# A hash-attention and SwiGLU kernel: weight words six pieces ahead, another order of the seven products, sums on x and preparing steps redistributed

## The chip, the cores and the metric

The kernel runs on one core of a Trainium2 chip. The metric is device time in microseconds (us), from the first to the last instruction; every execution of a program counts as one run. The engines of the core run beside each other and wait for one another through semaphores: TensorE (PE in the profile) multiplies, VectorE (DVE) and ScalarE (ACT) do elementwise work and empty the matmul banks (PSUM), GpSimd (POOL) and SyncE (SP) mainly issue DMA transfers.

## The reference

Two stages, cut to what matters. First an attention in which a query sees only the keys that have the same 6-bit hash; then a SwiGLU feed-forward block on the result.

```python
q, k, v: (4, 8, 768, 64) float32      # batch, heads, positions, head size
q_bits = (q @ proj > 0);  k_bits = (k @ proj > 0)        # 6 bits each
scores = where(bucket(q_bits) == bucket(k_bits), q @ k.T / 8, -1e9)
attn   = softmax(scores) @ v
x      = attn as (3072, 512)           # heads side by side
g      = x @ w_gate                    # (512, 1536)
out    = (g * sigmoid(g) * (x @ w_val)) @ w_out          # (1536, 512)
```

The input weights of the feed-forward block are float64; the program receives them as pairs of 32-bit words.

## The kernel before

The program is recorded in one order per engine, so what stands earlier in the Python loop stands earlier on its engine. Four things are interleaved.

**Attention.** The work is cut into 16 pairs of heads (four per batch), each in two halves of the queries: a *unit* is one half of one pair. For every unit TensorE makes the scores of six blocks of keys (the hash bits are multiplied on top of the scores in the same bank), ScalarE takes the exponential, VectorE adds the weights up (`add`, L485 and L489), and TensorE multiplies with v (`attend`). In the first half of a pair the next pair's q and k are transposed, in the second half its hash bits are made: ScalarE takes signs (L389), VectorE scales the k bits (L391). In the first four pairs (batch one) nothing else is multiplied; from the fifth pair on each unit also holds a part of the feed-forward block of the batch before.

**Preparing the weights.** The float64 weights come in 36 pieces of 512 KB (`words`). ScalarE scales both words of a piece (L282, L283), VectorE puts the float32 together in three steps (`narrow`), and after four pieces eight sums (`form`, L328) make the operands of a Strassen product, which go to memory and come back when they are wanted. One *preparing step* is one VectorE instruction of this chain. `load_words` keeps four pieces ahead; `words_tile` says where each piece lands, in space that is used otherwise later.

```python

    spots = [hid[:, half, m].rearrange("p f q -> p (f q)") for half in range(2) for m in range(2)]
    early = [as_words(t[:, 0 : 2 * PIECE]) for t in spots]
    early.append(as_words(part(2 * PIECE, at=down_at + 8 * BL)))
    middle = [as_words(t[:, NFP // 2 * HQ : NFP // 2 * HQ + 2 * PIECE]) for t in spots]
    late = [as_words(part(2 * PIECE, at=stage_at + i * 2 * PIECE)) for i in range(4)]

    def words_tile(i):
        if i < 12:
            return early[i % 5]
        if i < 24 and i % 6 < 4:
            return middle[i % 6]
        if i >= 24 and i % 6 not in (2, 3):
            return late[i % 6 // 4 * 2 + i % 2]
        return wraw.tile([P, PIECE, 2], I32, tag="words", name="words")

    def load_words(done, queue=nc.gpsimd):
        for i in range(len(words), len(pieces)):
            if i - done > 4:
                break
            words[i] = words_tile(i)
            queue.dma_start(words[i].rearrange("p f w -> p (f w)"), pieces[i][1])
...
    def scale_to(count):
...
        for i in range(progress["scaled"], min(count, free, len(pieces))):
            t, w = words[i], pieces[i][0]
...
            nc.scalar.activation(w, t[:, :, 1].bitcast(FP32), AF.Copy, scale=2.0**-112)
            nc.scalar.activation(t[:, :, 0], top, AF.Copy, scale=2.0**-13 * (1 + 2.0**-17))
...
    def scale_ahead():
        i = progress["piece"]
        scale_to(i + 3)
```

**Up.** x @ w_gate and x @ w_val are made as Strassen products: seven products in place of eight, from sums and differences of the quarters of x and of the weights. `first` holds the eight VectorE differences on x. One `step` is one product for the gate (g = 0) or for the value (g = 1), so 14 steps make a part of the up stage, and one unit holds one such part. Three banks for each g (a, b, c) take the products; products that share a bank add up in it, and what has to be used in between is copied out by ScalarE (L605) or added by VectorE (`plus`, L551). A finished gate tile goes through `gate`: tanh on ScalarE (L533), then VectorE (L534, L538).

```python
    def gate(t, g):

        th = t if t is not g else ffn.tile([P, HQ], FP32, tag="th", name="th", bufs=1)
        nc.scalar.activation(th, g, AF.Tanh, scale=0.5)
        return lambda: nc.vector.scalar_tensor_tensor(out=t, in0=th, scalar=1.0, in1=g,
                                                      op0=ALU.add, op1=ALU.mult)
...
            def step(at):
                n, g = divmod(at, 2)
                my = now[g]
                if at == 0:
                    for name in "cba":
                        for w in range(2):
                            now[w][name] = bank("up")[:, 0:HQ]
                    while first:
                        first.pop(0)()
                block, to, xs = (
                    (A11, "a", [x[j][:, lo] for j in range(2)]),
                    (S1, "b", [x[j][:, hi] for j in range(2)]),
                    (S2, "a", [t2[:, j] for j in range(2)]),
                    (A12, "c", [x[2 + j][:, lo] for j in range(2)]),
                    (S3, "a", [t3[:, j] for j in range(2)]),
                    (S4, "b", [x[2 + j][:, hi] for j in range(2)]),
                    (A22, "a", [t4[:, j] for j in range(2)]),
                )[n]
                w = places[g][:, block, :].rearrange("p (j m) -> p j m", m=P)
                c = my[to]
                product(c, [(w[:, j], xs[j]) for j in range(2)], n in (0, 1, 3))
                spot = ((0, 0), (1, 1), (0, 1), (0, 0), (1, 1), (0, 1), (1, 0))[n]
                if n < 3:
                    nc.scalar.copy(tile_of(g, spot), c)
                elif n < 6:
                    plus(my[spot], my[spot], c)
                    c = my[spot]
                while later and later[0][0] <= at:
                    later.pop(0)[1]()
                if n >= 3 and g == 0:
                    then = gate(tile_of(0, spot) if n == 6 else c, c)
                elif n >= 3:
                    then = lambda: gated(hidden(f + spot[0], spot[1]), now[0][spot], c)
                if n >= 3:
                    later.append((at + (1 if n == 6 else 2), then))
                if n in (3, 6):
                    bring(k0 + 2 + g, n // 6)
                while at == 13 and later:
                    later.pop(0)[1]()

```

**Down** (`po` in the profile) multiplies the gated tiles with w_out, again in seven products; its atoms have size 2.

The loop over units mixes all of this:

```python
    for u in range(0, N, NCH):
        n, half, _ = units[u]
        gating = u >= LATE
...
        for c in range(NCH):
            score(u + c)
            if u == 0 and c in (0, 1, 2, 4):
                prepare_pair(1)
                finish(rest)
            if c == 1 and half == 0 and 0 < n <= NP:
                total(n - 1)
            if c:
                add(u + c)
        if n <= NP:
            finish(waiting)
        if not gating and half == 0:
            steps = front(n + 1)
        if not gating and u > 0:
            prepare_pair(2)
        scale_ahead()
        for c in range(NCH):
            attend(u + c)
        if half == 1 and n + 2 < len(pairs):
            load(n + 2)
        if not gating:
            prepare_pair(2 if u > 0 else 4)
        finish(first)
        prepare_on(2)
        finish(rest)
        prepare_on(2)
        if half == 1 and n >= NP:
            total(n)
        prepare_on(0 if u == LATE else 4 if half or gating else 6)
        if not gating:
            continue
...
        credit += 14 if n < 2 * NP else 15.75
        end = True
        part = 0
        while atoms and (credit > 0 or not end):
            size, atom, end = atoms.pop(0)
            credit -= size
            atom()
            part += size
            if part >= 8:
                finish(waiting)
                if u + NCH == N:
                    finish(first)
            if part < 11:
                prepare_on(size)
            if part > 5:
                scale_ahead()
            for _ in range(size):
                if chores:
                    step = chores.pop(0)
                    chores.extend(step and step() or [])
```

`finish(waiting)` puts the normalisation of a pair's result in (L524); `finish(rest)` puts the k scaling in (L391); `chores` are the next pair's transposes or hash signs, one for each step. `gating` is true from the fifth pair on.

Of the kernel before, what the change touches and what calls it, by code (L numbers as in the profile page):

```python
# [10 lines left out]
I32 = mybir.dt.int32  # L11
# [7 lines left out]
def kernel(  # L19
# [224 lines left out]
    def as_words(t):  # L244
        return t.bitcast(I32).rearrange("p (f w) -> p f w", w=2)

    spots = [hid[:, half, m].rearrange("p f q -> p (f q)") for half in range(2) for m in range(2)]
    early = [as_words(t[:, 0 : 2 * PIECE]) for t in spots]
    early.append(as_words(part(2 * PIECE, at=down_at + 8 * BL)))
    middle = [as_words(t[:, NFP // 2 * HQ : NFP // 2 * HQ + 2 * PIECE]) for t in spots]  # L250
    late = [as_words(part(2 * PIECE, at=stage_at + i * 2 * PIECE)) for i in range(4)]

    def words_tile(i):
        if i < 12:
            return early[i % 5]
        if i < 24 and i % 6 < 4:
            return middle[i % 6]
        if i >= 24 and i % 6 not in (2, 3):
            return late[i % 6 // 4 * 2 + i % 2]
        return wraw.tile([P, PIECE, 2], I32, tag="words", name="words")  # L260

    def load_words(done, queue=nc.gpsimd):
        for i in range(len(words), len(pieces)):
            if i - done > 4:
                break
            words[i] = words_tile(i)
            queue.dma_start(words[i].rearrange("p f w -> p (f w)"), pieces[i][1])

    progress = {"late": False, "piece": 0, "scaled": 0, "blocks": 0}
# [86 lines left out]
    def prepare_on(n):  # L356
        for _ in range(n):
            next(preparing, None)

    load_words(-3, nc.sync)  # L360
    for name, queue in (("q", nc.sync), ("k", nc.gpsimd), ("v", nc.sync)):
        fetch(1, name, queue)
    load_words(-1)


    T = {}
# [186 lines left out]
    def up_strassen(x, b, first):  # L553
# [14 lines left out]
        def both(i):  # L568


            f = 2 * i
            k0 = b * NG + 2 * i
            now = [{}, {}]
            later = []

            def tile_of(g, spot):
                m, half = spot
                t = gate_tile() if g == 0 else hidden(f + m, half)
                now[g][spot] = t
                return t  # L580
# [9 lines that stand above are left out]
                        first.pop(0)()  # L590
                block, to, xs = (
                    (A11, "a", [x[j][:, lo] for j in range(2)]),
                    (S1, "b", [x[j][:, hi] for j in range(2)]),
                    (S2, "a", [t2[:, j] for j in range(2)]),
                    (A12, "c", [x[2 + j][:, lo] for j in range(2)]),
                    (S3, "a", [t3[:, j] for j in range(2)]),
                    (S4, "b", [x[2 + j][:, hi] for j in range(2)]),
                    (A22, "a", [t4[:, j] for j in range(2)]),
                )[n]
                w = places[g][:, block, :].rearrange("p (j m) -> p j m", m=P)  # L600
                c = my[to]
                product(c, [(w[:, j], xs[j]) for j in range(2)], n in (0, 1, 3))
                spot = ((0, 0), (1, 1), (0, 1), (0, 0), (1, 1), (0, 1), (1, 0))[n]
                if n < 3:
                    nc.scalar.copy(tile_of(g, spot), c)  # L605
                elif n < 6:
                    plus(my[spot], my[spot], c)
                    c = my[spot]
                while later and later[0][0] <= at:
                    later.pop(0)[1]()  # L610
                if n >= 3 and g == 0:
                    then = gate(tile_of(0, spot) if n == 6 else c, c)
                elif n >= 3:
                    then = lambda: gated(hidden(f + spot[0], spot[1]), now[0][spot], c)
                if n >= 3:
                    later.append((at + (1 if n == 6 else 2), then))
                if n in (3, 6):
                    bring(k0 + 2 + g, n // 6)
                while at == 13 and later:
                    later.pop(0)[1]()  # L620

            for n in range(2 * NB):
                atoms.append((1, lambda n=n: step(n), n == 2 * NB - 1))
# [95 lines left out]
    def finish(todo):  # L719
        while todo:  # L720
            todo.pop(0)()
# [5 lines left out]
    for u in range(0, N, NCH):  # L727
# [26 lines left out]
        if not gating:  # L754
            prepare_pair(2 if u > 0 else 4)
        finish(first)
        prepare_on(2)
        finish(rest)
        prepare_on(2)
        if half == 1 and n >= NP:  # L760
            total(n)
        prepare_on(0 if u == LATE else 4 if half or gating else 6)
        if not gating:
            continue
        chores = []
# [10 lines left out]
        while atoms and (credit > 0 or not end):  # L776
# [4 lines left out]
            if part >= 8:  # L781
                finish(waiting)
                if u + NCH == N:
                    finish(first)
            if part < 11:
                prepare_on(size)
            if part > 5:
                scale_ahead()
# [41 lines left out]
```

## Time and profile before

| what | value |
|---|---|
| time, median of 3 runs | 1019.64 us (1019.41 to 1020.11) |
| span of the profiled run | 1017.2 us |
| mean granted TensorE clock | 0.998 |
| time of batch one (before the first up product) | 0 to 122.1 us |
| VectorE busy between 20 and 120 us | 84.9 us |
| one unit's scores, 36 instructions | 5.04 us |
| one unit's attend, 24 instructions | 4.04 us |
| one part of up, 14 steps in 56 instructions | 18.26 us |

An instruction group in the profile is named by line, engine and operation, then output <- input by the program's names, then its count; what stands in square brackets is the idle time of the engine just before it and what ended that idle time. `L551 DVE TENSOR_TENSOR c<-c,up` is thus the sum of a bank and a tile of the gate. In stretches of time, each engine's busy microseconds are given with its count of instructions, then the TensorE clock as a share of full speed, the busy share of the DMA engines and the GB/s they moved. Scores are `sc`, the products with v are `av`, the row sums `sum`, the hash products `hps`, transposes `tps`.

### The profile page before, as it was taken

The page shows a single profiled execution, that of the slowest core. Times are in us where ns is not written, and L with a number is a line of the kernel's source. Part 1 is how long each engine was busy: PE and PEld are TensorE (multiplying, and loading weights), DVE is VectorE, ACT ScalarE, POOL GpSimd, SP SyncE. Part 2 cuts the span into 40 slices and gives each one's busy share as a digit, 9 for nine tenths or more (in the row PEclk, how much of TensorE's full clock was granted, in tenths as well). Part 3 has the DMA queues.
Part 4 walks back from the last instruction along what each step waited for, and adds up shares of the span by engine and source line. Part 5 has one row for each costly group of instructions (what it writes and reads, how often), then busy time and mean ns, then how long its engine had stood idle before and what let it go on. Part 6 is the DMA issues. An engine that isn't in the chain of part 4 may idle for free.

```text
span 1017.2 us, 12536 instructions
## 1 busy us (share of the span) xinstructions
PE 1002.9 (99%) x4597; PEld 603.2 (59%) x4597; DVE 576.6 (57%) x959; ACT 419.7 (41%) x921; POOL 98.8 (10%) x192
## 2 busy tenths in 40 slices
PE   9998999999999999999999999999999999999998
PEld 4443455545566775555557676555555787555687
DVE  5789988789684515655455453545557341434421
ACT  7776746475532414535342422535435201222200
POOL 2221222311000000000000000000000000111000
PEclk9999999999999999999999999999999999999999
DMA  7774886674323123333430304242222011323001
GB/s 226 217 245 157 218 242 216 196 221 118 89 73 73 33 52 98 94 101 92 104 90 30 73 22 104 88 101 66 72 81 81 21 37 48 107 83 114 31 26 37
DMA packets 120029, 106.21 MB, mean 104 GB/s; under 512 B 89024, under 2 KB 103360, under 8 KB 119968
## 3 DMA queue, kind: packets, MB, share of 16 engines
q0 software_dynamic: 19104, 73.28, 22.4%
q1 hardware_dynamic: 100064, 31.94, 14.0%
q8 instruction: 36, 0.59, 0.2%
q10 hardware_dynamic: 800, 0.20, 0.1%
q14 instruction: 25, 0.20, 0.1%
HBM read 81.79 MB, written 17.30 MB: 97 GB/s over the span
## 4 chain that ended last, share of the span: by engine, by line
PE 86%; DVE 7%; DMA 2%; SPq 2%; issue 2%; ACT 1%; POOL 0%; DVEq 0%; POOLq 0%
PE up L547 40%; PE po L547 21%; PE sc L457 12%; PE av L471 10%; SPq L515 2%; DMA wo<-wo 1%; DVE acc L489 1%; DVE wo L510 1%; PE sum L502 1%; PE hps L404 1%; DVE room L328 1%; DMA hid<-in_moe_w_val_dram 1%; DVE room L299 1%; PE hps L396 1%; DVE xc L551 1%
## 5 line engine op out<-in xcount | busy, mean ns | idle before, releaser
L547 PE MATMUL up<-xT,room 128*128 128x384 f32 x768 | 263.8, 490 | 1.9 <-DVE xT L551 1.9
L547 PEld LDWEIGHTS up<-xT,room 128*128 128x128 f32 x768 | 143.8, 190 | 112.2 <-issue 14.9
L547 PE MATMUL up<-xc,room 128*128 128x384 f32 x576 | 197.6, 486 | 1.1 <-DVE c L551 1.1
L457 PE MATMUL sc<-qT,kT 64*128 64x384 f32 x768 | 161.8, 496 | 0.4 <-DVE c L534 0.4
L547 PEld LDWEIGHTS up<-xc,room 128*128 128x128 f32 x576 | 109.3, 190 | 77.8 <-DVE c L551 1.7
L551 DVE TENSOR_TENSOR c<-c,up 128x384 f32<-128x384 f32 x72 | 39.7, 551 | 180.0 <-PE up L547 179.5
L489 DVE TENSOR_TENSOR acc<-acc,A 128x768 f32<-128x768 f32 x128 | 122.7, 958 | 15.0 <-ACT A L460 1.6
L313 POOL DMA_DIRECT2D room<-ram x96 | 51.8, 540 | 714.0 <-PE up L547 706.5
L460 ACT ACTIVATE A<-sc 128x384 f32<-128x384 f32 x256 | 105.6, 493 | 6.3 <-PE sc L457 6.2
L457 PEld LDWEIGHTS sc<-qT,kT 64*128 64x128 f32 x768 | 68.5, 187 | 52.9 <-issue 47.9
L677 ACT COPY o<-po 128x256 f32<-128x256 f32 x48 | 17.9, 372 | 197.8 <-PE po L547 197.8
L471 PE MATMUL av<-A,vraw 128*64 128x384 f32 (+1 forms) x512 | 88.2, 486 | 0.0
L533 ACT ACTIVATE th<-c 128x384 f32<-128x384 f32 x72 | 37.6, 523 | 115.4 <-DVE c L534 94.4
L551 DVE TENSOR_TENSOR o<-o,po 128x256 f32<-128x256 f32 x36 | 15.1, 420 | 121.0 <-PE po L547 91.9
L457 PE MATMUL sc<-qb,kb 64*128 64x384 bf16 x384 | 65.7, 324 | 4.9 <-DVE kb L391 4.9
L460 ACT ACTIVATE room<-sc 128x384 f32<-128x384 f32 x128 | 54.4, 490 | 37.3 <-PE sc L457 37.3
L547 PE MATMUL po<-room,hid 128*128 128x256 f32 x288 | 66.2, 379 | 1.5 <-DVE o L551 1.5
L547 PE MATMUL po<-wo,hid 128*128 128x256 f32 x288 | 66.9, 382 | 0.0
L547 PE MATMUL po<-wo,room 128*128 128x256 f32 x288 | 66.3, 380 | 0.0
L605 ACT COPY c<-up 128x384 f32<-128x384 f32 x72 | 34.4, 478 | 75.8 <-PE up L547 75.6
L471 PEld LDWEIGHTS av<-A,vraw 128*64 128x64 f32 x512 | 36.7, 137 | 46.0 <-issue 44.8
L547 PEld LDWEIGHTS po<-wo,hid 128*128 128x128 f32 x288 | 54.1, 190 | 12.1 <-issue 4.9
(110 smaller groups left out, 1004.0 us busy)
## 6 DMA issues: line engine op xcount, KB each, us to landing
room<-ram POOLq DMA_DIRECT2D x48, 512.0 KB, 4.8
room<-ram POOLq DMA_DIRECT2D x48, 384.0 KB, 3.8
vraw<-in_v_dram SPq DMA_DIRECT2D x16, 384.0 KB, 3.3
ram<-room POOLq DMA_DIRECT2D x12, 512.0 KB, 4.6
out_dram<-o SPq DMA_DIRECT2D x48, 128.0 KB, 1.7
qraw<-in_q_dram SPq DMA_DIRECT2D x48, 96.0 KB, 3.2
hid<-in_moe_w_val_dram POOLq DMA_DIRECT2D x9, 512.0 KB, 6.8
acc<-acc SPq DMA_DIRECT2D x96, 48.0 KB, 1.9
```

The source lines that it names most:

```text
L299: nc.vector.scalar_tensor_tensor(out=wi, in0=hi, scalar=-(1 << 31), in1=wi, op0=ALU.bitwise_and, op1=ALU.bitwise_or)
L313: nc.gpsimd.dma_start(places[k % 2][:, PARTS[go], :], ram[k % NG][:, PARTS[go], :])
L457: nc.tensor.matmul(sc[h], x["k", n][rows, ks], x["q", n][rows, qs], start=start, stop=not start)
L460: nc.scalar.activation(weights(u)[:, h, 0:HQ], sc[h], AF.Exp, scale=SCALE)
L471: nc.tensor.matmul(ps[h * D : (h + 1) * D, 0:width], raws["v", n][:, h, c, :], a[:, h, 0:width], start=c == 0, stop=c == NCH - 1)
L489: nc.vector.tensor_tensor(acc[n, half], acc[n, half], a[:, :, 0:HQ], op=ALU.add)
L515: nc.sync.dma_start(t[at : at + BLOCK, half, :], r[g : g + BLOCK, :])
L533: nc.scalar.activation(th, g, AF.Tanh, scale=0.5)
L547: nc.tensor.matmul(ps, a, x, start=start and i == 0, stop=i == len(pairs_) - 1, skip_group_check=True)
L551: nc.vector.tensor_tensor(o, a, b, op=op)
L605: nc.scalar.copy(tile_of(g, spot), c)
L677: nc.scalar.copy(o, c)
```

## The change

Four things are changed. The weight words are loaded up to six pieces ahead (in the last eight pieces four), into eight homes in turn for the first twelve pieces, where there were five; a list `homes` takes the place of `words_tile`. In the up stage the product A12, which needs none of the differences on x, comes second instead of fourth, ahead of the products that need them (S1, S2), so that VectorE has time for the differences; it is finished as soon as it is added to the copy of A11, so its gate follows at once. In the last unit of the attention the eight differences on x are put in two per part instead of all at once. And the preparing steps are moved: in batch one every unit has ten (second halves had eight), all after the k scaling; in the later units there are three in place of four behind the row sums and one part fewer has them.

```diff
--- before.py
+++ after.py
@@ -246,24 +246,20 @@
 
     spots = [hid[:, half, m].rearrange("p f q -> p (f q)") for half in range(2) for m in range(2)]
     early = [as_words(t[:, 0 : 2 * PIECE]) for t in spots]
-    early.append(as_words(part(2 * PIECE, at=down_at + 8 * BL)))
     middle = [as_words(t[:, NFP // 2 * HQ : NFP // 2 * HQ + 2 * PIECE]) for t in spots]
     late = [as_words(part(2 * PIECE, at=stage_at + i * 2 * PIECE)) for i in range(4)]
-
-    def words_tile(i):
-        if i < 12:
-            return early[i % 5]
-        if i < 24 and i % 6 < 4:
-            return middle[i % 6]
-        if i >= 24 and i % 6 not in (2, 3):
-            return late[i % 6 // 4 * 2 + i % 2]
-        return wraw.tile([P, PIECE, 2], I32, tag="words", name="words")
+    beside = as_words(part(2 * PIECE, at=down_at + 8 * BL))
+    turn = [None] * 2 + [beside]
+    homes = [(early + middle)[i % 8] for i in range(12)]
+    homes += middle + turn + middle + turn + late + turn + late[:3]
 
     def load_words(done, queue=nc.gpsimd):
         for i in range(len(words), len(pieces)):
-            if i - done > 4:
+            if i - done > (6 if i < 28 else 4):
                 break
-            words[i] = words_tile(i)
+            words[i] = homes[i]
+            if words[i] is None:
+                words[i] = wraw.tile([P, PIECE, 2], I32, tag="words", name="words")
             queue.dma_start(words[i].rearrange("p f w -> p (f w)"), pieces[i][1])
 
     progress = {"late": False, "piece": 0, "scaled": 0, "blocks": 0}
@@ -357,10 +353,10 @@
         for _ in range(n):
             next(preparing, None)
 
-    load_words(-3, nc.sync)
+    load_words(-5, nc.sync)
     for name, queue in (("q", nc.sync), ("k", nc.gpsimd), ("v", nc.sync)):
         fetch(1, name, queue)
-    load_words(-1)
+    load_words(-3)
 
 
     T = {}
@@ -590,29 +586,30 @@
                         first.pop(0)()
                 block, to, xs = (
                     (A11, "a", [x[j][:, lo] for j in range(2)]),
+                    (A12, "c", [x[2 + j][:, lo] for j in range(2)]),
                     (S1, "b", [x[j][:, hi] for j in range(2)]),
                     (S2, "a", [t2[:, j] for j in range(2)]),
-                    (A12, "c", [x[2 + j][:, lo] for j in range(2)]),
                     (S3, "a", [t3[:, j] for j in range(2)]),
                     (S4, "b", [x[2 + j][:, hi] for j in range(2)]),
                     (A22, "a", [t4[:, j] for j in range(2)]),
                 )[n]
                 w = places[g][:, block, :].rearrange("p (j m) -> p j m", m=P)
                 c = my[to]
-                product(c, [(w[:, j], xs[j]) for j in range(2)], n in (0, 1, 3))
-                spot = ((0, 0), (1, 1), (0, 1), (0, 0), (1, 1), (0, 1), (1, 0))[n]
-                if n < 3:
+                product(c, [(w[:, j], xs[j]) for j in range(2)], n in (0, 1, 2))
+                spot = ((0, 0), (0, 0), (1, 1), (0, 1), (1, 1), (0, 1), (1, 0))[n]
+                if n in (0, 2, 3):
                     nc.scalar.copy(tile_of(g, spot), c)
                 elif n < 6:
                     plus(my[spot], my[spot], c)
                     c = my[spot]
                 while later and later[0][0] <= at:
                     later.pop(0)[1]()
-                if n >= 3 and g == 0:
+                done = n in (1, 4, 5, 6)
+                if done and g == 0:
                     then = gate(tile_of(0, spot) if n == 6 else c, c)
-                elif n >= 3:
+                elif done:
                     then = lambda: gated(hidden(f + spot[0], spot[1]), now[0][spot], c)
-                if n >= 3:
+                if done:
                     later.append((at + (1 if n == 6 else 2), then))
                 if n in (3, 6):
                     bring(k0 + 2 + g, n // 6)
@@ -754,12 +751,11 @@
         if not gating:
             prepare_pair(2 if u > 0 else 4)
         finish(first)
-        prepare_on(2)
         finish(rest)
-        prepare_on(2)
+        prepare_on(4)
         if half == 1 and n >= NP:
             total(n)
-        prepare_on(0 if u == LATE else 4 if half or gating else 6)
+        prepare_on(0 if u == LATE else 3 if gating else 6)
         if not gating:
             continue
         chores = []
@@ -781,8 +777,8 @@
             if part >= 8:
                 finish(waiting)
                 if u + NCH == N:
-                    finish(first)
-            if part < 11:
+                    finish([first.pop(0) for _ in range(min(2, len(first)))])
+            if part < 10:
                 prepare_on(size)
             if part > 5:
                 scale_ahead()
```

## The prediction

> **What bounds the kernel now.** I read the page first (shares of the span), then TensorE's waits, then the chain that ended last, and last the timelines of the places where TensorE waits. The page:
>
> ```profile
> PE 1002.9 (99%) x4597; PEld 603.2 (59%) x4597; DVE 576.6 (57%) x959; ACT 419.7 (41%) x921; POOL 98.8 (10%) x192
> PE 86%; DVE 7%; DMA 2%; SPq 2%; issue 2%; ACT 1%; POOL 0%; DVEq 0%; POOLq 0%
> ```
>
> TensorE has 1017.2 - 1002.9 = 14.3 us of idle time, and the change removes no matmul. So whatever it gains is gap, and whatever it loses is new gap. TensorE's waits name the gaps:
>
> ```profile
> PE sc L457 <- DVE kb L391: 4.9, 2, 3.6
> PE up L547 <- DVE xT L551: 1.9, 1, 1.9
> PE po L547 <- DVE o L551: 1.5, 1, 1.5
> PE up L547 <- DVE c L551: 1.1, 1, 1.1
> PE sc L457 <- DVE c L534: 0.4, 1, 0.4
> ```
>
> Columns: total, times, longest, in us. They sum to 9.8 us; the rest of the 14.3 is head and tail. The 3.6 us gap (84 to 87.5 us) costs more than itself, as the stretches after it show (TensorE's busy time and count first; clock, DMA share and GB/s last):
>
> ```profile
> 84.00:88.00 4.00, 0.53 (x4) 0.39 (x6) 3.77 (x7) 2.70 (x6) 0.00 (x0) 0.97 0.79 311
> 88.00:92.00 4.00, 4.00 (x22) 1.29 (x20) 3.80 (x7) 1.58 (x4) 1.48 (x2) 0.60 0.08 23
> ```
>
> The clock is 0.60 for 4 us. From the bits product to the first score of the next position the timeline has 4.36 us (87.47 to 91.83), for the same work 2.77 us elsewhere (59.97 to 62.74): 1.6 us lost. All that could be won is thus 9.8 + 1.6 = 11.4 us, 1.1%. From 230 us on nearly everything in the chain is TensorE, back to back.
>
> [...] at 84.3 us ScalarE has waited 5.0 us for one piece of weights, and the sign operations behind it are late with it. [...] the trace has 0.60 after the gap of 3.6 us and 1.00 around the gap of 1.9 us at 125 us. [...] That is the crux here: the new order of the seven products leaves less room between an eviction and the product that adds into the same bank.
>
> **Part by part.**
>
> *Words six ahead, and the k bits scaled straight after hashing.* The gap of 3.6 us is a chain: ScalarE waits for words, VectorE's preparing step for ScalarE, the k scaling (L391) stands behind that step, the scores wait for it. Words loaded earlier break the first link. The move of two preparing steps behind the k scaling breaks the third. Worth at most 4.9 + 1.6 = 6.5 us. But batch one then carries 10 steps in each second half in place of 8: 8 more in all, at about 0.56 us (a piece is 3 steps in 2.0 us; a block is 4 pieces and 8 sums of 0.40, so 11.2 us for 20 steps), 4.5 us of VectorE, where it has idle only some 15 us between 20 and 120 us (84.9 busy of 100). I count 65%: **-4.2 us**.
>
> *Product without differences second.* At 125 us the second product (S1) waits 1.9 us for x's differences; A12 needs none and gives 2.6 us (two groups of 1.29) in that place. With the wait at the end of this unit: **-2.3 us**.
>
> *Two sums on x per part, last batch.* The 1.5 us at 830 us is an o sum queued behind eight differences (8 x 0.47 = 3.8 us) on VectorE. Two at a time fit between products of 2.6 us: **-1.4 us**. The 1.1 us wait at 228 us goes too, since units hold fewer steps: **-1.1 us**. Sum of gains: -9.0 us.
>
> *What the new order costs.* S2 and S3 both add into bank "a", and S3 must wait until ScalarE has copied S2. Before, A12 stood between them; now S3 comes right behind: only the other group's product (1.29 us) lies between. Second, A12 now ends early, so its tanh stands on ScalarE ahead of the copies of S1 and S2, and in the second half of a pair ahead of the hash signs too. The order of the changed program shows it: copy, copy, tanh, four k signs, copy S1, two q signs, copy S1, two q signs, copy S2. A steady unit of before is the base (the timeline of ScalarE; start, duration):
>
> ```profile
> 459.14 0.48 ACT L605 COPY hid<-up 128x384 f32<-128x384 f32 x1 [0.81 <-PE up L547]
> 461.41 0.48 ACT L605 COPY c<-up 128x384 f32<-128x384 f32 x1 [1.79 <-PE up L547]
> 461.79 1.16 ACT L389 ACTIVATE kb<-hps,columns 32x384 bf16<-32x384 f32 x2
> 462.97 0.48 ACT L605 COPY hid<-up 128x384 f32<-128x384 f32 x1
> 463.46 1.17 ACT L389 ACTIVATE kb<-hps,columns 32x384 bf16<-32x384 f32 x2
> 464.65 0.48 ACT L605 COPY c<-up 128x384 f32<-128x384 f32 x1
> 466.84 1.16 ACT L389 ACTIVATE qb<-hps,columns 32x384 bf16<-32x384 f32 x2
> 468.03 0.52 ACT L533 ACTIVATE th<-c 128x384 f32<-128x384 f32 x1
> ```
>
> Spacings on ScalarE: copy 0.38, tanh 0.43, a pair of signs 1.17, a piece's two scalings 1.14. Put 0 at 461.41, where step 2's product can be evicted; step k's can at 1.29 (k-2). After the change: sum on VectorE and tanh at 0.63, k signs 1.06 to 3.40, copy S1 to 3.78, q signs to 4.95, copy to 5.33, q signs to 6.50, then the copy of S2, done 0.48 later; S3 starts 0.06 after that, at 7.04. It would have started at 6.25 (467.66). So **0.8 us per second-half unit**. Seven have no scaling in between (the last of the first block, three in each of two more): 7 x 0.78 = **+5.5 us**.
>
> In the first block's units scalings come in between as well (counted in the changed program, from the start of the up stage):
> - Unit 2: two pieces, 2 x 1.14, so 0.78 + 2.3 = **+3.1 us**.
> - Unit 4: one piece among the k signs and three behind S1, 4.6; and the tanh comes 0.9 later, as the reciprocal and five preparing steps stand before its sum on VectorE: 0.8 + 4.6 + 0.9 = **+6.3 us**.
> - Unit 1: VectorE does eight differences, six preparing steps and a transpose before A12's sum. From the base:
>
> ```profile
> 125.29 1.02 DVE L551 TENSOR_TENSOR xc<-xT 128x384 f32<-128x384 f32 x2
> 131.42 0.97 DVE L422 STREAM_TRANSPOSE qT<-qraw 128x768 f32<-128x768 f32 x1
> 134.87 0.55 DVE L551 TENSOR_TENSOR c<-c,up 128x384 f32<-128x384 f32 x1
> ```
>
> 125.3 + 3.8 + 4.0 + 1.0 = 134.1; tanh at 134.7; two copies of S1 to 135.9; three pieces, 3.4, to 139.3; copy of S2 to 139.8. S3 could start at 122.1 + 8 x 1.29 = 132.4: **+7.4 us**.
> - Units 3 and 5: at most one piece behind S1, which fits: +0.2 us.
>
> Sum: 5.5 + 3.1 + 6.3 + 7.4 + 0.2 = 22.5 us. Two of these gaps are surely, a third maybe, long enough for the slow clock: 2 x 1.6 = +3.2 us. The last batch's up stage has neither signs nor scalings, and the copy there is in time (0.54 us after its product against 1.09 allowed).
>
> Total: 1019.6 - 9.0 + 22.5 + 3.2 = 1036.3 us.
>
> **Rivals.** (1) *Gaps go, nothing comes*: 1019.6 - 11.4 = 1008 us. For it: each part names a gap that the profile shows. Against: it takes the copy of S2 to be prompt, while ScalarE's order puts 7 us of work before it. (2) *Batch one becomes VectorE's or the DMA queues'*: six pieces ahead is 2 MB more in the first 120 us, where the DMA share is already 0.5 to 0.98, and VectorE gets 4.5 us more; the gains of batch one vanish and 2 to 5 us of new waits come: about 1040 to 1043 us with the stalls above, 1022 without. (3) *The stalls come but are smaller*, if the words' scalings were done earlier by the longer lead: then only the 5.5 us and part of units 1 and 4 remain, about 1024 us.
>
> **Range.** My sum gives 1036; I shade it to 1035, since unit 1 rests on the longest chain. Mechanism right and the first-block stalls halved: 1026. Everything at its worst: 1043. Range 1024 to 1042. Over 2% slower (1040.0) wants the stalls at full size and no gain in batch one: 0.18. Over 2% faster (999) is more than all gaps: 0.005.
>
> **What would show it.** TensorE should newly wait in "up" for ScalarE's copy (L601 there), some ten waits, nine of them in second halves and the longest in units 1 and 4, 6 to 7 us each, with clock under 1 after them; the waits for kb, xT and o should be gone or small. The first tanh of each up unit should stand ahead of the third copy. If no wait for that copy shows, the new order is free and rival 1 holds.

## The result, and the profile after

The changed kernel takes 1063.45 us (median of four runs, 1063.08 to 1065.11), the kernel before 1019.88 us beside it: ratio 1.043, 95% interval 1.041 to 1.045. It is 43.6 us slower; predicted were 1035 us and a range up to 1042.

The page of the changed kernel, busy time of the engines and shares of the chain that ended last:

```profile
PE 1014.6 (96%) x4597; PEld 604.6 (57%) x4597; DVE 582.9 (55%) x959; ACT 418.3 (39%) x921; POOL 99.5 (9%) x192
PE 82%; DVE 6%; ACT 5%; DMA 3%; SPq 1%; issue 1%; POOL 0%; DVEq 0%; ACTq 0%
```

The same 4597 matmuls are busy 11.7 us longer (1014.6 for 1002.9), and the span of 1061.3 us leaves 46.7 us of idle time where there were 14.3. The longer busy time goes with a lower granted clock, 0.982 for 0.998. ScalarE's share of the chain has gone from 1% to 5%. What TensorE waited for, in total, times, longest (us):

```profile
PE up L543 <- ACT c L601: 23.1, 10, 6.8
PE sc L453 <- DVE kb L387: 13.2, 3, 6.2
PE tps L375 <- DMA qraw<-in_q_dram: 3.2, 1, 3.2
...
PE up L543 <- DVE xT L520: 1.0, 1, 1.0
```

Line numbers are four lower than in the kernel before: L601 is the copy that was L605, L387 the k scaling that was L391. The first line is the new one that the prediction described. The second is an old one (4.9 us before) that should have gone and has nearly tripled. The waits for `o` and for `c` (1.5 and 1.1 us) are gone.

Where the 44 us of span lie, by the start of the first matmul of a stage:

| stretch | before | after | difference | the prediction's terms for it |
|---|---|---|---|---|
| batch one, up to the first up product | 122.1 | 140.7 | +18.6 | -4.2 |
| first block's up stages, to the first `po` | 174.9 | 194.8 | +19.9 | +17.6 (7.4 + 3.1 + 6.3 + 0.2 + one steady unit 0.8 + clock 3.2 - 2.3 - 1.1) |
| the rest | 720.2 | 725.8 | +5.6 | +3.3 (six steady units 4.7 - 1.4) |

So the stall in "up" came nearly as worked out, and batch one, which should have won a little, lost 18.6 us. Two chains have to be shown.

**The copy behind the tanh and the scalings.** The timeline of the changed kernel in unit 1 (start, duration, then the instruction; in brackets the idle time before it), ScalarE first, TensorE's matmul last:

```profile
154.64 0.52 ACT L529 ACTIVATE th<-c 128x384 f32<-128x384 f32 x1 [10.54 <-DVE c L547]
155.07 0.46 ACT L601 COPY c<-up 128x384 f32<-128x384 f32 x1
...
155.80 0.67 ACT L278 ACTIVATE room<-hid 128x512 f32<-128x512 f32 x1
...
158.57 0.67 ACT L279 ACTIVATE hid<-hid 128x512 int32<-128x512 uint16 x1
159.14 0.47 ACT L601 COPY c<-up 128x384 f32<-128x384 f32 x1
...
159.66 4.78 PE L543 MATMUL up<-xc,room 128*128 128x384 f32 x8 [6.83 <-ACT c L601]
```

ScalarE stood still for 10.54 us ahead of a tanh whose input VectorE had not made, although the copies of finished products stood behind it. Then came the copies of S1, three pieces of weights (155.80 to 159.14), and only then the copy of S2 that the product S3 waited for. So ScalarE kept to the program's order, although the products S1 and S2 were finished by 152.83 us, where TensorE's gap of 6.83 us begins. The eight matmuls after it took 4.78 us, at a granted clock of 0.51 (159.7 to 163.7 us), where the same group takes 2.85 elsewhere.

**Batch one: a late broadcast, and everything behind it.** The same timeline, 77 to 103 us. SyncE (SPq) sends the row sums' reciprocals out in eight transfers of 48 KB (`wo<-wo`), GpSimd (POOL) moves blocks of weights, VectorE normalises with what arrives:

```profile
77.40 6.87 SPq L511 DMA_DIRECT2D wo<-wo  x8
77.75 1.09 POOL L309 DMA_DIRECT2D room<-ram  x2 [3.56 <-issue]
...
80.88 1.08 POOL L263 DMA_DIRECT2D hid<-in_moe_w_val_dram  x2
...
85.07 0.62 DVE L520 SCALAR_TENSOR_TENSOR xT<-xT,e,wo 128x384 f32<-128x384 f32 x1 [2.64 <-DMA wo<-wo]
...
90.61 0.62 DVE L520 SCALAR_TENSOR_TENSOR xT<-xT,e,wo 128x384 f32<-128x384 f32 x1 [4.92 <-DMA wo<-wo]
...
102.08 0.55 DVE L387 TENSOR_SCALAR kb<-kb,columns 128x384 bf16<-128x384 bf16 x2
...
102.45 0.50 PE L453 MATMUL sc<-qb,kb 64*128 64x384 bf16 x2 [6.17 <-DVE kb L387]
```

VectorE lost 7.56 us at two normalisations, did the steps and sums that stand next, and reached the k scaling at 102.08; TensorE had waited 6.17 us. The windows of time around it (busy time and count of each engine, then clock, DMA share, GB/s) show the second half of the price:

```profile
96.00:100.00 4.00, 0.28 (x2) 0.00 (x0) 3.78 (x5) 0.05 (x1) 0.00 (x0) 0.84 0.16 54
100.00:104.00 4.00, 1.55 (x6) 0.78 (x8) 3.76 (x8) 0.87 (x2) 0.00 (x0) 0.50 0.00 0
```

VectorE is full, TensorE nearly empty, and its clock at half when work comes back. In all VectorE waited 16.7 us for `wo` in the first 142 us, against 8.1 us before; the broadcast took 5.4 us in the median from issue to landing, against 2.9.

### The profile page after: what moved, and what is told of

It is laid out like the page before. It is cut to its first block, busy times and chain, and to the rows that moved or that the text cites. A ratio compares the mean times of both kernels' runs of the same rounds, so it can differ in the third digit from the quotient of the medians.

```text
span 1061.3 us, 12573 instructions
## 1 busy us (share of the span) xinstructions
PE 1014.6 (96%) x4597; PEld 604.6 (57%) x4597; DVE 582.9 (55%) x959; ACT 418.3 (39%) x921; POOL 99.5 (9%) x192
## 4 chain that ended last, share of the span: by engine, by line
PE 82%; DVE 6%; ACT 5%; DMA 3%; SPq 1%; issue 1%; POOL 0%; DVEq 0%; ACTq 0%
PE up L543 39%; PE po L543 21%; PE sc L453 12%; PE av L467 8%; DVE acc L485 2%; DMA wo<-wo 1%; SPq L511 1%; ACT qb L385 1%; DMA qraw<-in_q_dram 1%; PE sum L498 1%; DMA words<-in_moe_w_gate_dram 1%; ACT A L456 1%; DVE room L295 1%; DVE wo L506 1%; PE hps L400 1%
## 5 line engine op out<-in xcount | busy, mean ns | idle before, releaser
L543 PE MATMUL up<-xT,room 128*128 128x384 f32 x768 | 260.1, 490 | 1.0 <-DVE xT L520 1.0
L543 PE MATMUL up<-xc,room 128*128 128x384 f32 x576 | 201.7, 498 | 23.1 <-ACT c L601 23.1
L453 PE MATMUL sc<-qb,kb 64*128 64x384 bf16 x384 | 64.3, 329 | 13.2 <-DVE kb L387 13.2
L481 DVE SCALAR_TENSOR_TENSOR acc<-room 128x768 f32<-128x768 f32 x32 | 30.4, 950 | 59.2 <-ACT room L456 59.2
```

What stands on the lines that cost most here:

```text
L453: nc.tensor.matmul(sc[h], x["k", n][rows, ks], x["q", n][rows, qs], start=start, stop=not start)
L481: nc.vector.scalar_tensor_tensor(out=acc[n, half], in0=weights(u - 1)[:, :, 0:HQ], scalar=S * EPS / P, in1=a[:, :, 0:HQ], op0=ALU.add, op1 ...
L543: nc.tensor.matmul(ps, a, x, start=start and i == 0, stop=i == len(pairs_) - 1, skip_group_check=True)
```

## The experiments

The letters in the expectations: F, ScalarE's strict order makes the stall in "up"; G, the distance of one product between S2 and S3 does; D, the words six ahead make batch one slow; N, VectorE's waiting at the normalisation does; P, the phase of the blocks of weights against the broadcast does; V, the eight extra steps are too much work for VectorE; L, the waits in "up" come only from words and batch one being late. Times stand beside runs of the kernel before on the same chip; in brackets the ratio to it with its 95% interval. The runs of a, of e and f, and of g are from three chips, on which the kernel before takes 1019.5 to 1020.0 us.

### The parts one by one

**a1, the product order alone** (the hunk of the up stage in the diff above, on the kernel before):

```diff
                     (A11, "a", [x[j][:, lo] for j in range(2)]),
+                    (A12, "c", [x[2 + j][:, lo] for j in range(2)]),
                     (S1, "b", [x[j][:, hi] for j in range(2)]),
                     (S2, "a", [t2[:, j] for j in range(2)]),
-                    (A12, "c", [x[2 + j][:, lo] for j in range(2)]),
```

> Only the new order of the seven products on the kernel before. Theory F (ScalarE's strict order: A12's tanh, signs and scalings stand ahead of the copy of S2): TensorE waits about 20 to 23 us in up for that copy, the first up product still starts near 122 us, time 1036 to 1044 us. Rival L (the up waits in the changed kernel came from words and batch one being late): hardly any wait for the copy, 1017 to 1022 us.

Measured 1043.74 us (1.0236, 1.0221 to 1.0252), and TensorE's longest item:

```profile
PE up L547 <- ACT c L605: 20.6, 11, 6.8
```

The order costs 24.1 us by itself, with batch one as before (first up product at 121.8): L falls. The sum of the waits is near the changed kernel's 23.1, their places are not: units 1 to 4 wait 1.95, 3.56, 1.70 and 6.79 us here. In unit 1 no scaling lies between the copies of S1 and S2; the 6.83 us of the changed kernel's unit 1 need the moved words or steps as well.

**a2, the words six ahead alone** (the hunks of `homes` and `load_words`):

```diff
-            if i - done > 4:
+            if i - done > (6 if i < 28 else 4):
```

> Only the words six pieces ahead (eight homes). Theory D (more word transfers in flight make the row sums' broadcast and q land later, and VectorE stands behind the broadcast): first up product at 130 to 142 us, VectorE waits over 12 us for the broadcast in batch one, time 1028 to 1040 us. Rival V (the eight extra preparing steps overload VectorE): first up product at 116 to 123 us, time 1013 to 1021 us.

1022.96 us (1.0037, 1.0025 to 1.0048). The first up product starts at 127.8, 5.7 us late, but VectorE's wait for the broadcast is 7.7 us, against 8.1 before: D falls. (The time lies in neither of the two ranges.) What is new is a wait of 3.6 us for q at the transposes near 25 us. With eight homes GpSimd issues four loads of 512 KB back to back at 12.4 us, beside a q (12.6) and a v (14.3); with five homes one is issued there, and the next only at 20.7, when the first piece is used up. The kb wait, 4.9 us before, is still 4.6: the earlier words don't break the chain that the prediction wanted broken.

**a3, the preparing steps alone:**

```diff
-        prepare_on(2)
         finish(rest)
-        prepare_on(2)
+        prepare_on(4)
...
-        prepare_on(0 if u == LATE else 4 if half or gating else 6)
+        prepare_on(0 if u == LATE else 3 if gating else 6)
...
-            if part < 11:
+            if part < 10:
```

> Only the moved preparing steps (ten per unit in batch one, all after the k scaling). Rival V: first up product at 130 to 142 us, time 1028 to 1040 us. Theory D: within 5 us of before, 1015 to 1024 us, the gap of 3.6 us for kb smaller.

1036.01 us (1.0159, 1.0142 to 1.0176). TensorE's waits of this run:

```profile
PE sc L457 <- DVE kb L391: 13.3, 3, 6.9
PE up L547 <- DVE xT L551: 4.8, 1, 4.8
```

Here is most of the loss of batch one: the first up product starts at 135.0, 12.9 us late, the kb wait is within 0.1 us of the changed kernel's 13.2, and neither words nor order are touched; VectorE waits 21.2 us for the broadcast. With the 5.7 us of a2 these 12.9 us make the 18.6 of the table. So far V has foretold the result; e1 and e2 decide on it.

**a4, the changed kernel with the old order:**

> The changed kernel with the old order of the products (words, steps and two sums per part stay). Theory F: no wait for the copy in up, batch one as slow as in the changed kernel, 1036 to 1042 us; F's share and batch one's add up to the 43 us. If the two parts feed each other (late words also lengthen the up waits), the sum of this loss and a1's is well under 43 us.

1036.00 us (1.0162, 1.0147 to 1.0177). The order's 24.1 and this run's 16.4 make 40.5 of the 43.6 us: the two losses nearly add. The words, 3.3 us in a2, add nothing here to the 16.4 us of a3: the first up product comes at 140.7, 5.7 us after a3's, and the rest of the run is 5.4 us shorter, 1.5 us of it by the wait for `o`, which the two sums per part remove. (No run has those sums alone.)

### What in the moved steps

**e3, two more steps in each second half, nothing else:**

```diff
-        prepare_on(0 if u == LATE else 4 if half or gating else 6)
+        prepare_on(0 if u == LATE else 4 if gating else 6)
```

> Only the two more preparing steps in batch one's second halves; two steps still stand ahead of the k scaling; later units as before. Theory P and rival V both: most of the loss of the moved-steps kernel, 1028 to 1038 us. If the loss comes from moving the k scaling or from the later units: 1018 to 1023 us.

1037.66 us (1.0175, 1.0159 to 1.0190), kb wait 15.4 us, broadcast wait 21.7 us. What makes the loss is ten steps in every unit, not their new place.

**e4, the k scaling ahead of the steps, nothing else** (the first four lines of a3's diff):

> Only the k scaling ahead of the preparing steps, with the number of steps as before. If the move is what helps (the gap of 3.6 us and its slow clock go): 1012 to 1017 us, no kb wait over 1.5 us. If the order of these few instructions doesn't matter, since what holds VectorE lies further ahead: 1018 to 1022 us.

1020.47 us (1.0006, 0.9997 to 1.0015). The kb wait falls only from 4.9 to 3.8 us, and 3.2 us of waits for the reciprocal (`av` for `wo`) come in its place. The gain that the prediction counted on (up to 6.5 us with the words) isn't there even alone.

**e1, a3 with batch one's normalisation behind the preparing steps:**

```diff
-        if n <= NP:
+        if n == NP:
             finish(waiting)
...
         if not gating:
+            finish(waiting)
             continue
```

> The moved steps alone, with batch one's normalisation put behind the preparing steps on VectorE, so that nothing stands behind its wait for the broadcast. Theory N (VectorE waits in order for the row sums' broadcast, 21 us in the moved-steps kernel, and preparing, adds and k scaling wait behind it): kb waits fall from 13.3 to under 5 us, first up product by 124 us, 1015 to 1022 us. Rival V (ten steps are too much VectorE work for a unit): still over 8 us of kb waits and 1030 us or more.

1020.72 us (1.0006, 0.9999 to 1.0013). kb wait 1.2 us, batch one over at 119.6 us, before even the kernel before (122.1). N holds and V falls: with the steps of a3 untouched, 15.3 us go when VectorE no longer stands at the normalisation while the broadcast travels. (TensorE waits 5.5 us at the first differences on x, whose input is now normalised last; before it was 1.9.)

**e2, a3 with five steps fewer in the very first unit.** Twenty steps are one block of weights, and ten per unit make one block per pair. So with ten everywhere, each block is complete at the same place of each pair; five fewer once shift all blocks by half a unit.

```diff
-        prepare_on(0 if u == LATE else 3 if gating else 6)
+        prepare_on(0 if u == LATE else 3 if gating else 6 if u else 1)
```

> The moved steps alone, with five steps fewer in the very first unit. Ten steps per unit make one weight block of 20 steps per pair, so each block's transfers fall at the same place of a pair. Theory P (this place is the broadcast, whose transfers then compete with them): shifted by five steps, VectorE's waits for the broadcast fall from 21 to under 14 us, time 1018 to 1028 us. Rival V or N without P: 1032 to 1038 us, as the moved-steps kernel.

1016.03 us (0.9967, 0.9954 to 0.9980): 0.3% faster than before, with as many steps per unit from the second unit on as in a3, and no wait for kb. (By the program batch one has 75 steps here, 80 in a3 and 72 before. That the five left out are not the cause is seen from e1, which has all 80 and loses 1 us.) The broadcast's 32 transfers took from issue to landing (us, minimum, median, maximum), first in a3, then in e2:

```profile
DMA to landing us min/median/max: 4.2/5.5/9.0
```

```profile
DMA to landing us min/median/max: 1.9/2.1/4.5
```

In a3's timeline GpSimd starts its stores among SyncE's transfers:

```profile
70.13 7.27 SPq L515 DMA_DIRECT2D wo<-wo  x8
...
71.25 0.77 POOL L321 DMA_DIRECT2D ram<-room  x1
```

In e2's GpSimd starts nothing between 63.9 and 73.6 us, while SyncE sends:

```profile
65.86 5.01 SPq L515 DMA_DIRECT2D wo<-wo  x8
...
73.59 0.58 POOL L330 DMA_DIRECT2D ram<-room  x1 [9.71 <-DVE room L328]
```

The same holds for the other broadcasts: in the changed kernel and in a3 all four have block or word transfers of GpSimd started within 2 us of their start, in e2 none has one started during it. P holds as to the place of the blocks: with GpSimd's transfers (128 to 512 KB each) started at other times, the median landing of the 48 KB ones falls from 5.5 to 2.1 us, and VectorE's wait for them from 21.2 to 4.5. That the two compete for the DMA engines is P's assumption and not shown, as no run moved GpSimd's transfers alone.

### What in the product order

**f1, the order of a1 with A12's tanh behind the copies of S2:**

```diff
+                if n == 1 and g == 0:
+                    later.append((7, lambda: later.insert(0, (8, gate(c, c)))))
-                if done and g == 0:
+                elif done and g == 0:
                     then = gate(tile_of(0, spot) if n == 6 else c, c)
...
```

> The kernel before with the new product order alone, but the tanh of A12's gate is put on ScalarE behind the copies of S2 instead of ahead of the copies of S1. Theory F (ScalarE does strictly what comes first in its order, and an instruction that waits for its input holds the copies behind it; the tanh waits for VectorE's sum): TensorE's waits for the copy fall from 20.6 us (order alone) to what the scalings and hash signs between the copies leave, 3 to 9 us; unit 1 falls from 6.8 to under 3.5 us; the steady second halves lose their 0.96 us; time 1024 to 1032 us. Rival G (the distance of one product of 1.29 us between S2 and S3 is itself too short for a copy): the waits of the steady units stay near 1 us each and the time stays above 1038 us.

1033.45 us (1.0135, 1.0111 to 1.0159), 10.3 us under a1 and 1.5 us above the range. TensorE's longest item:

```profile
PE up L547 <- ACT c L605: 7.6, 3, 3.5
```

The waits for the copy fall from 20.6 to 7.6 us, and those of the seven steady units are gone. G, which wanted 1 us each to stay, falls as the main cause. (The 6.8 us that the expectation gives to unit 1 is unit 4's in a1; it falls to 3.5, and unit 1's 1.95 to nothing.) What was won partly went to another wait, for a gate's last sum on VectorE: 3.3 us, 1.5 in a1.

**f2, f1 with the scalings behind the copies of S2 as well** (and one piece more ahead of `attend`):

```diff
-            if part > 5:
+            if part > 8:
                 scale_ahead()
```

> As the run with the later tanh, and the weights' scalings are issued on ScalarE only in the last parts of a unit's up stage, behind the copies of S2; one more piece is scaled ahead of attend, so that VectorE's steps find their input. Theory F: waits for the copy under 3 us in all; time 1016 to 1023 us, if no wait of VectorE for scaled words takes their place. Rival G: 1032 us or more, with waits for the copy left in the second halves.

1024.06 us (1.0038, 1.0025 to 1.0050), 9.4 us less again; one wait of 1.3 us for the copy is left. F has the wait for the copy right; the time is 1 us above the range. The waits for kb (4.8 us, batch one as before) and for the gate's sum (3.5 us) remained, with the clock at 0.60 and 0.50 after their longest gaps.

### Both mended

**f3, f2 with a3's steps, e2's shift and two differences per part; words four ahead. f4, the changed kernel with the same mending (words six ahead).**

> The two mended parts together: new product order with tanh and scalings behind the copies, the preparing steps behind the k scaling as in the changed kernel but five fewer in the very first unit (so that no block of weights is completed just before the row sums' broadcast), and two differences per part in the last batch; words four pieces ahead as before. If the two theories (F for ScalarE's order, P for the phase of the blocks of weights) are right and add up: batch one ends at about 121 us, waits for the copy under 3 us, none for kb, none for the first differences on x; time 1009 to 1015 us, faster than before by 0.5 to 1%. If they collide (scalings too late for the moved steps), 1016 to 1024 us.

1016.04 us (0.9964, 0.9951 to 0.9977).

> The changed kernel whole (words six ahead too) with the same mending: tanh and scalings behind the copies, five fewer steps in the first unit. Its difference to the run with words four ahead is what the six-ahead loads cost or bring now: the q transposes at 25 us wait 3 us for q, so 3 us slower is expected, 1012 to 1018 us. If the words six ahead were of use elsewhere, it equals or beats that run.

1022.62 us (1.0027, 1.0019 to 1.0035), 18 runs from 1019.1 to 1024.8. Both missed. f3 is no faster than e2 with the old order, although it has the two sums per part besides; 1.7 us of that are a slow stretch after a gap of 2.60 us at 117 us, which e2 has as well and passes at full clock (the last section comes back to this). And six ahead costs 6.6 us where 3 were expected. (f4 and g3 also scale one piece more ahead than f3.) In f4's profile GpSimd issues the four loads in one go, at 12.68 us.

**g3, f4 with the sixth piece in the first one's home**, so that GpSimd must hold it, and what follows, until the first piece is used up (in the kernel before a load into that home was issued at 20.69 us, after 7.49 us of waiting for VectorE):

```diff
-    homes = [(early + middle)[i % 8] for i in range(12)]
-    homes += middle + turn + middle + turn + late + turn + late[:3]
+    homes = early + [middle[0], early[0], middle[2], middle[3]]
+    homes += [middle[1]] + early[1:] + [beside, middle[0], middle[2], middle[3]]
+    homes += turn + middle + turn + late + turn + late[:3]
```

> The changed kernel whole with the mending (as the run that took 1022.6 us), words still up to six ahead, but the sixth piece lands where the first lies, so that GpSimd can't issue it, nor what follows, until the first piece is used up: two val loads less beside the first q and v. If the late q is all that six-ahead costs: the wait of the transposes for q (3.2 us) goes, and the time is that of four ahead, 1015 to 1017 us, with a narrow spread. If six-ahead costs something elsewhere (loads beside the attention's own): 1018 to 1021 us.

1016.86 us (0.9970, 0.9960 to 0.9979), 1016.3 to 1017.2: no wait for q, 5.8 us less than f4, and 0.8 us from f3, within the intervals. So six ahead costs through those first loads, and brings nothing that shows later. Of the 5.8 us the profiled run of f4 (1020.5 us) shows 3.2 as the wait for q; what the runs up to 1024.8 us had besides wasn't profiled and stays open.

**g1 and g2: f3's steps split 12 and 8 between a pair's halves, with the old order (g1) and the mended new one (g2).** In f3 TensorE waits 6.0 us for a reciprocal that stands behind the second half's steps.

```diff
-        prepare_on(0 if u == LATE else 3 if gating else 6 if u else 1)
+        prepare_on(0 if u == LATE else 3 if gating else (4 if half else 8) if u else 1)
```

> The product order of the kernel before, words four ahead, the k scaling ahead of the steps and five steps fewer in the first unit, two differences per part in the last batch, and of the 20 steps of a pair in batch one 12 in the first half and 8 in the second (10 and 10 in the runs before), so that the next unit's reciprocal has less in front of it. If the steps stand in front of the reciprocal: the waits for it fall from 5.6 us to under 2 us, and without the 1.5 us wait in the last batch the time is 1010 to 1013 us. If moving the steps only brings the broadcast or the k scaling into the way again: 1015 us or more.

1013.73 us (0.9947, 0.9932 to 0.9962), the fastest kernel of this study, though the wait for the reciprocal fell only to 4.3 us, not under 2, and the time is 0.7 us above the range.

> The mended kernel (new product order with tanh and scalings behind the copies, phase of the blocks shifted, two differences per part) with the steps of a pair in batch one split 12 and 8 in place of 10 and 10. Waits for the reciprocal from 6.0 to under 2 us, time 1010 to 1013 us. Against the run with the old product order: if A12 in second place is worth the 1.9 us wait for the first differences, this one is 1 to 2 us faster; if the copy of S2 takes it back, they agree within 1 us.

1015.86 us (0.9968, 0.9956 to 0.9979); reciprocal 4.1 us. The new order, mended, is 2.1 us *slower* than the old one, an outcome that was not named. No wait in the lists accounts for that. By the timelines a steady second-half unit, from its first up product to the next scores, takes 19.24 us in g1 (452.42 to 471.66) and 19.56 in g2 (453.24 to 472.80). The 0.32 us lie in S2 and S3, which take 5.48 us (462.06 to 467.54) where two such products take 5.16 in g1: S3 still comes a little before the copy of S2. ScalarE's order shows why:

```profile
463.14 1.16 ACT L389 ACTIVATE qb<-hps,columns 32x384 bf16<-32x384 f32 x2
464.33 0.48 ACT L605 COPY c<-up 128x384 f32<-128x384 f32 x1
```

Two hash signs still stand ahead of the copy. S2's first product ends near 463.35 (462.06 and 1.29), S3 could start at 464.64 (462.06 and 2.58), and the copy ends at 464.81. First-half units have the same distance between S2 and S3, but no signs, and they take the same time in both runs: 18.25 us in g1 (424.32 to 442.57), 18.26 in g2 (425.13 to 443.39). So this rest is ScalarE's order again (F), and nothing is left for G; no run has the signs behind the copy too. Seven such units make the 2.2 us by which g2 falls back between 265 us (0.27 us behind) and 848 us (2.43).

## Why the prediction was wrong, point by point

**Right: the chain in "up".** Ten waits for the copy, the longest in units 1 and 4, were foretold, and the sum was 22.5 us; measured are 23.1. By unit: unit 1 6.83 (predicted 7.4), unit 2 3.31 (3.1), unit 4 6.18 (6.3), seven steady units 1.05 and six times 0.96 (0.78 each). Counting instructions of known duration along ScalarE's order gave this, and f1 and f2 confirm its links: the tanh is worth 13.0 us of waits, the scalings 6.3. Small terms were undersized. A steady unit is 1.22 us longer than before (20.46 for 19.24): 0.96 us are the wait, and 0.26 us more are lost around it. (The 13.0 and 6.3 us are measured from a1 on, whose waits lie in other places, as said there.)

**The clock, too small.** The sum had two slow stretches at 1.6 us; how many gaps bring one was my estimate, for which the kernel before shows a clock of 0.60 after its gap of 3.60 us and 1.00 after that of 1.88. All three long gaps in "up" were followed by one (clock 0.51, 0.57 and 0.53 in the 4 us after them), and the groups of eight matmuls took 4.78, 4.54 and 4.69 us for 2.85: 1.9, 1.7 and 1.8, together 5.5 us for 3.2. The second of these followed a gap of 3.31 us, which I had called "a third maybe". A gap of about that size can also leave the clock alone, as the last section shows.

**The step that failed: "I count 65%: -4.2 us".** It weighed 8 more VectorE steps, 4.5 us, against 15 us that VectorE had idle between 20 and 120 us, and took the k scaling's new place as a gain. Measured is +18.6 us in that stretch, 12.9 from the moved steps (a3) and 5.7 from the words (a2):
- The added steps alone (e3) bring the first up product 14.0 us late (136.1) and cost 18 us in all, not because VectorE ran out of time but because they brought the blocks of weights to ten steps a unit, in step with the broadcast, for which VectorE waits 21.7 us. An average of idle time over 100 us can't show that; the order of GpSimd's transfers against SyncE's could have. Two runs, one with all the steps and the normalisation later (e1), one with the blocks half a unit off (e2), take the loss away.
- The k scaling ahead of the steps is worth nothing by itself (e4).
- The words six ahead don't end the kb wait (4.6 us in a2 for 4.9) and make TensorE wait 3.6 us for q in a2, 3.2 in the changed kernel. That transfer the sum had not at all.

**Rival 2 had the place and not the size.** It named batch one, VectorE and the DMA queues, with "2 to 5 us of new waits" over a lost gain. But it counted bytes and busy time, and the queue it meant was the weights' own. Its "2 MB more in the first 120 us" did not come: by 122 us both kernels have issued 20 loads of words. The 48 KB broadcast on another queue, at which VectorE stood 16.7 us in the changed kernel with its later work behind it, was missing.

**Gains that came and gains that didn't.** The waits for `o` and `c` (1.5 and 1.1) went as predicted; but that the one for `c` went because units hold fewer steps is not shown, as e2 has the same fewer steps and still waits 1.1 us. The 1.9 us wait for the first differences went too, with A12 in second place; yet as a reason for the new order it is not enough: mended as far as g2, with the signs still ahead of the copy, it loses 2.1 us to the old order. The upper end of the range was "everything at its worst" for the stalls, with no more than a few microseconds for batch one.

## What to carry to other kernels

When a change moves work on an engine that isn't the bound, look at what that work triggers (here transfers) and at what travels at that moment with an engine waiting for it that has more work behind the wait (here VectorE, 21.2 us in a3); a share of idle time says nothing about that. Issue what is ready ahead of what still waits for its input: on ScalarE the copies of finished banks ahead of the tanh, worth 13.0 us of waits here (f1), on VectorE the preparing steps ahead of the normalisation, worth 15.3 us (e1). Check it in the order of the program, not in the order of the mathematics. Where two periods meet (20 steps a block, two units a pair), try shifting one against the other before cutting work: here it was worth 20 us and cost one number.

## What of the hardware was not expected

A slow clock also followed gaps much shorter than the 3.60 us of the kernel before. The windows of g1 and of g2 after a gap of 1.96 and 1.95 us, with the same work before it (clock third from the end):

```profile
116.90:120.90 4.00, 4.00 (x16) 1.59 (x18) 3.63 (x4) 2.30 (x5) 0.00 (x0) 0.58 0.28 71
```

```profile
116.80:120.80 4.00, 3.97 (x24) 1.64 (x24) 3.67 (x4) 3.53 (x7) 0.00 (x0) 1.00 0.30 75
```

One ran at 0.58 and did 16 matmuls, the other at full clock and did 24. The profiles of all 17 kernels together have 74 gaps of 1.25 us or more on TensorE after 20 us. In the 4 us after each, the mean clock was 1.00 for all 35 gaps up to 1.95 us, and 0.50 to 0.61 for all 14 from 4.26 us on. Of the 25 between, 1.96 to 3.82 us, 18 were followed by 0.50 to 0.68 and seven by 1.00, among them a gap of 3.82 us (a4). e2 and f3 have the same gap of 2.60 us at 117 us, one with 1.00 after it and one with 0.61: the eight `av` products behind it take 1.52 us in e2 and 2.00 in f3. What decides between the two the profiles don't show. For a sum, an estimate from these counts: a gap between 2 and 4 us carries the 1.6 to 1.9 us of a slow stretch in about three cases of four (18 of 25), a longer one in all (14 of 14).
